# Transfer landing times in a build-time planner: two queues that share one rate, and the loads of units 3 to 5 put around the four quarters of w_out

## The chip, the cores and the metric

The kernel runs on one core of a Trainium2 chip. The metric is the device time in microseconds (us) of one execution; eight timed runs of the kernel before have a median of 397.88 us and lie between 396.91 and 398.88. The profile is one further reading of such an execution, with its own time.

## The reference

Attention with a squared relu, followed by a feed-forward layer with a squared relu:

```python
def _attn_ref(q, k, v):                       # q, k, v: (8, 12, 448, 64), float32
    scores = np.matmul(q, k.transpose(0, 1, 3, 2)) / np.sqrt(64)
    attn = np.maximum(scores, 0.0) ** 2 / 448
    return np.matmul(attn, v)

x = attn_out.transpose(0, 2, 1, 3).reshape(3584, 768)
h = x @ w_in                                  # w_in: (768, 2048)
r = np.maximum(h, 0.0)
out = (r * r) @ w_out                         # w_out: (2048, 768), out float32
```

## The kernel before, in words

**Units and rounds.** The 8 batches of 12 heads are cut into 24 units of four heads. For a unit, q and k are each loaded as one tile `raw` of 448 KB (float32), cast to half precision into a tile `blk`, and turned (transposed) into a tile `qkt`. v is loaded with a cast on the way into a tile `vs`. A unit has 7 rounds; a round multiplies 64 rows of k with all of q (four matmuls, L406, into `sp`), takes the relu with a scale (`rel`: L433 on VectorE or L436 on ScalarE) and squares it (`at`: L440 on ScalarE or L442 on GpSimd). When the seven rounds of a unit are there, 28 matmuls with v (L471) follow, and their results are copied to `xt`. In a batch's feed-forward part, L533 multiplies `xt` with w_in, L522 (ScalarE) and L517 (VectorE) form the squared relu `g`, and L682 or L747 multiply g with w_out and store.

**Units 0 to 2, the first batch.** They come first and are cut into two column parts, so that the first product with w_in (L582, four groups of six matmuls, one for each quarter of w_in) can start early. The q and k of units 1 and 2 are loaded by GpSimd into a g buffer. Up to planned time 45 the planner puts small idle matmuls (L885) where TensorE would have nothing to do.

**w_in and w_out.** Each comes in four quarters of 768 KB (counted in half precision), loaded by GpSimd (L380 and L385). The quarters of w_out are `w2[0][0]`, `w2[0][1]`, `w2[1][0]`, `w2[1][1]`. After the first batch's feed-forward part, `combine_w2` forms four differences of them, t1 to t4, each in two halves (L708 on GpSimd, L711 on VectorE); they serve a product of two row blocks with seven half-size multiplications in place of eight (L747). Every half of t1 waits for all four quarters, and t2 to t4 come behind t1.

**Who issues what.** SyncE's queue carries the raw tiles (L302), the transposing transfers of units 6 and up (L361) and the output stores (L628). GpSimd's queue carries v (L375), w_in and w_out. A queue issues in order; an instruction that has to wait holds all that stand behind it on its engine.

**The planner.** All operations are first added to a `Plan`, with costs, due times, and sometimes a time `after` which they may start. `Plan.run` simulates engines, buffers and transfers, always takes the ready operation with the earliest due time for an engine that is free, and emits the instructions in that order. The chip then runs each engine's instructions in the emitted order, and waits only on semaphores: a planned time exists only in the planner. Where a raw load has `gate=True`, a tiny memset on GpSimd (L299) stands ahead of it, and through it the load can't start before GpSimd gets there. The planner has no model of the port that VectorE and GpSimd share beyond L711 and L726 waiting for a free GpSimd. Before the change, all transfers run one after the other through a single server:

```python
if size:
    dma = max(dma, begin + 1.2) + size / 390e3
    op.end = dma + 1.0
```

**The buffers that matter here.** There are 4 raw tiles, 3 blk, 6 qkt, 4 vs, 4 rel, 11 at, and 4 banks `mm` of PSUM. A raw tile is free for the next load when its cast (L325) is done; a blk tile when it has been turned.

Of the kernel before, what the change touches and what calls it, by code (L numbers as in the profile page):

```python
# [42 lines left out]
class Plan:  # L43
# [27 lines left out]
        return op  # L71

    def run(self):
        n_ops = len(self.ops)
        late: dict = {}
        for z, op in enumerate(self.ops):
            op.id = z
            op.wait = len(op.deps)
            op.ready = op.after
        for op in reversed(self.ops):  # L80
            if not op.fixed or op.alts[0][0] != "PE":
                took = min(a[2] for a in op.alts)
                if len(op.alts[0]) > 4 and op.alts[0][4]:
                    took = 7.0
                due = min([x.due for x in op.nexts] or [1e6]) - took - 0.1
                op.due = due if op.due is None else min(op.due, due)
        waiting: list = []
        for op in self.ops:
            if not op.wait:
                insort(waiting, (op.due, op.id, op))  # L90
        events = sorted({0.0} | {op.after for op in self.ops} | set(self.busy.values()))
        heapq.heapify(events)
        mode, dma, done = None, 0.0, 0
        last = None
        while done < n_ops:
            if not events:
                raise RuntimeError("no operation can go on")
            now = heapq.heappop(events)
            while events and events[0] <= now + 1e-9:
                heapq.heappop(events)  # L100
            again = True
            while again:
                again = False
                for eng in ("PE", "ACT", "DVE", "POOL", "SP"):
                    if self.busy[eng] > now + 1e-9:
                        continue
                    got = None
                    if eng == "PE" and last is not None and last.glue is not None:
                        soon = self.soon(last.glue)
                        if now < soon <= now + 0.45:  # L110
                            heapq.heappush(events, soon)
                            continue
                        if soon <= now:
                            got = waiting.index((last.glue.due, last.glue.id, last.glue)), (
                                last.glue.alts[0])
                    got = got or self.pick(eng, now, waiting)
                    if got is None:
                        if eng == "PE" and now < self.fill_until:
                            self.fill(now)
                            heapq.heappush(events, self.busy[eng])  # L120
                        continue
                    z, alt = got
                    op = waiting.pop(z)[2]
                    _, busy, took, emit, *rest = alt
                    begin = now
                    size = rest[0] if rest else 0
                    if eng == "PE":
                        last = op
                        begin += self.SWITCH.get((mode, op.mode), 0.0)
                        mode = op.mode  # L130
                        if now < self.cold:
                            busy, took = busy * 1.6, took * 1.6
                    if len(rest) > 1 and self.busy["POOL"] > now:
                        wait = self.busy["POOL"] - now
                        busy, took = busy + wait, took + wait
                    op.engine, op.start = eng, begin
                    op.end = begin + took
                    self.busy[eng] = begin + busy
                    if size:
                        dma = max(dma, begin + 1.2) + size / 390e3  # L140
                        op.end = dma + 1.0
                        if eng == "POOL":
                            self.sent += [op.end] * (2 if size == 458752 and took > 1.0 else 1)
                    if len(rest) > 1:
                        self.busy["POOL"] = max(self.busy["POOL"], self.busy[eng])
                    for b in op.bufs:
                        if b.tile is None:
                            slot = min(x for x in self.pools[b.pool] if x[0] <= now + 1e-9)
                            self.pools[b.pool].remove(slot)
                            b.tile, b.slot = slot[2], slot[1]  # L150
                    emit()
                    heapq.heappush(events, self.busy[eng])
                    seen = op.end + self.LAG[eng]
                    for b in op.bufs:
                        b.left -= 1
                        b.end = max(b.end, op.end + 0.07)
                        if not b.left:
                            self.pools[b.pool].append((b.end, b.slot, b.tile))
                            heapq.heappush(events, b.end)
                    for x in op.nexts:  # L160
                        x.wait -= 1
                        x.ready = max(x.ready, seen)
                        if not x.wait:
                            insort(waiting, (x.due, x.id, x))
                            heapq.heappush(events, x.ready)
                    done += 1
                    again = True
        return max(op.end for op in self.ops)

    def soon(self, op):  # L170

# [11 lines left out]
    def fill(self, now):  # L183

        free = [x for x in self.pools["mm"] if x[0] <= now + 1e-9]
        if len(free) > 1:
            slot = min(free)
            self.filler(slot[2])
            self.pools["mm"].remove(slot)
            self.pools["mm"].append((now + 0.2, slot[1], slot[2]))  # L190
        self.busy["PE"] = now + 0.11
# [26 lines left out]
def kernel(  # L218
# [68 lines left out]
    def load_qk(n, w, after=0.0, gate=False):  # L287
        b, u = divmod(n, NU)
        buf = Buf("raw")

        def tile_of():
            return buf.tile

        src = (q if w == "q" else k)[b, 4 * u:4 * u + 4].rearrange(
            "(f e) (p t) d -> (e p) f (t d)", e=2, t=TJ)
        deps = []
        if gate:
            deps.append(plan.add(
                [("POOL", 0.1, 0.1, lambda: nc.gpsimd.memset(buf.tile[0:1, 0, 0:1], 0.0))],  # L299
                bufs=[buf], after=after))  # L300
# [57 lines left out]
    def turn_dma(n, w, cast):  # L358
        op, blk, _ = cast
        to = Buf("qkt")  # L360
        done = plan.add([("SP", 1.3, 5.0, lambda: nc.sync.dma_start_transpose(  # L361
            out=to.tile, in_=blk.tile.rearrange("p t c -> p (t c)")), 1000000)], [op], [blk, to])
        qkt[n, w] = [done], to

    vst: dict = {}
# [583 lines left out]
    tile(1, rounds[1:2])  # L949
    for w_ in "kq":  # L950
        casts[3, w_] = cast_qk(3, w_, raws[3, w_])
        raws[4, w_] = load_qk(4, w_, 24.0, True)
    load_v(3, 26.0)
    w2_ops = [[load_w2(hf, z, 29.0 + 6.0 * hf + z) for z in range(2)] for hf in range(2)]
    for w_ in "kq":
        raws[5, w_] = load_qk(5, w_, 35.0, True)
    load_v(4, 36.0)
    for i in range(2, STREAM):
        tile(1, rounds[i:i + 1])
        if i % 4 == 3:  # L960
# [11 lines left out]
    def coming(n):  # L972
        return plan.now + 4.5 * (TJ * n - 2 * i) / 2

    skipped, chain = 0, None
    for i in range(STREAM // 2, NB):
        rs = [divmod(r, TJ) for r in range(max(STREAM, 2 * i), 2 * i + 2)]
        for n in range(NU, NUN):
            if i == max(STREAM // 2, TJ * (n - 2) // 2 + 1):
                if n > 5:  # L980
                    for w in "kq":
                        raws[n, w] = load_qk(n, w, coming(n) - 26.0)
                if n > 4:
                    load_v(n, coming(n) - 6.0)
            if i == max(STREAM // 2, (TJ * (n - 1) + 1) // 2 - 2) and n > 3:
                for w in "kq":
                    casts[n, w] = cast_qk(n, w, raws[n, w])
                if n < NPE:
                    for w in "kq":
                        turn_pe(n, w, casts[n, w])  # L990
                else:
                    for w in "kq":
                        turn_dma(n, w, casts[n, w])
# [60 lines left out]
```

## Time and profile before

| | |
|---|---|
| median of 8 timed runs | 397.88 us |
| profiled execution, its own time | 398.88 us |
| its span in the trace | 397.1 us (1.8 us lie around it) |
| TensorE busy | 382.4 us, 96% of the span |
| VectorE, ScalarE, GpSimd busy | 267.4, 279.9 and 175.9 us |
| mean granted TensorE clock | 0.991 |
| read from and written to HBM | 45.61 and 11.01 MB |

TensorE is busy nearly always, so what can be won or lost is what it does not work, and where it works at a lower clock. "Releaser" in the profile's rows is what ended an idle time. Times in the rows are counted from the start of the span.

### The profile page before, as it was taken

The page shows a single profiled execution, that of the slowest core. Times are in us where ns is not written, and L with a number is a line of the kernel's source. Part 1 is how long each engine was busy: PE and PEld are TensorE (multiplying, and loading weights), DVE is VectorE, ACT ScalarE, POOL GpSimd, SP SyncE. Part 2 cuts the span into 40 slices and gives each one's busy share as a digit, 9 for nine tenths or more (in the row PEclk, how much of TensorE's full clock was granted, in tenths as well). Part 3 has the DMA queues.
Part 4 walks back from the last instruction along what each step waited for, and adds up shares of the span by engine and source line. Part 5 has one row for each costly group of instructions (what it writes and reads, how often), then busy time and mean ns, then how long its engine had stood idle before and what let it go on. Part 6 is the DMA issues. An engine that isn't in the chain of part 4 may idle for free.

```text
span 397.1 us, 8331 instructions
## 1 busy us (share of the span) xinstructions
PE 382.4 (96%) x3298; PEld 202.0 (51%) x3298; DVE 267.4 (67%) x382; ACT 279.9 (70%) x417; POOL 175.9 (44%) x174
## 2 busy tenths in 40 slices
PE   8997996999999999999999999999999999999996
PEld 4543663444445544544555545544555445555563
DVE  2663888867688657767797655858686767355841
ACT  3985998699876788758878877879586876244111
POOL 7564579548474346448613645335411533000100
PEclk9998999899999999999999999999999999999999
DMA  9999999695937837667587596384263001220143
GB/s 192 191 235 252 267 240 169 113 191 118 235 70 191 192 69 154 165 166 118 126 182 172 119 196 151 73 205 118 45 129 81 2 1 30 62 50 1 41 115 85
DMA packets 69671, 52.72 MB, mean 133 GB/s; under 512 B 36864, under 2 KB 69632, under 8 KB 69632
## 3 DMA queue, kind: packets, MB, share of 16 engines
q1 hardware_dynamic: 53744, 38.61, 39.4%
q0 software_dynamic: 15296, 12.72, 22.0%
q10 hardware_dynamic: 592, 0.85, 0.6%
q8 instruction: 26, 0.43, 0.5%
q14 instruction: 13, 0.11, 0.1%
HBM read 45.61 MB, written 11.01 MB: 143 GB/s over the span
## 4 chain that ended last, share of the span: by engine, by line
PE 82%; DMA 8%; ACT 3%; DVE 2%; issue 2%; POOL 1%; POOLq 0%; DVEq 0%
PE mm L533 35%; PE mm L747 27%; PE sp L406 8%; PE mm L471 7%; DMA w<-in_moe_w_in_dram 6%; PE mm L682 3%; DMA g<-in_q_dram 2%; ACT rel L436 1%; DVE comb L726 1%; ACT g L522 1%; ACT at L440 1%; PE mm L582 1%; DVE g L517 1%; POOL g L315 1%; PE mm L345 1%
## 5 line engine op out<-in xcount | busy, mean ns | idle before, releaser
L533 PE MATMUL mm<-xt,w 128*128 128x448 f16 (+1 forms) x768 | 149.0, 346 | 0.0
L442 POOL TENSOR_TENSOR at<-rel 128x896 f16<-128x896 f32 (+1 forms) x48 | 77.8, 1622 | 108.9 <-ACT rel L436 82.4
L440 ACT ACTIVATE at<-rel 128x896 f16<-128x896 f32 (+1 forms) x120 | 109.6, 930 | 9.7 <-DVE rel L433 5.0
L517 DVE SCALAR_TENSOR_TENSOR g<-mm,g 128x448 f16<-128x448 f32 (+1 forms) x128 | 76.3, 604 | 52.3 <-ACT g L522 52.1
L433 DVE TENSOR_SCALAR rel<-sp 128x896 f32<-128x896 f32 (+3 forms) x87 | 90.9, 1048 | 27.8 <-PE sp L406 25.9
L533 PEld LDWEIGHTS <-w 128*128 128x128 f16 x768 | 72.3, 98 | 69.8 <-issue 11.4
L522 ACT ACTIVATE g<-mm 128x448 f16<-128x448 f32 (+1 forms) x128 | 67.1, 534 | 41.3 <-PE mm L533 40.5
L436 ACT ACTIVATE rel<-sp 128x896 f32<-128x896 f32 (+2 forms) x87 | 77.9, 900 | 7.9 <-PE sp L406 6.4
L325 POOL CAST blk<-raw 128x896 f16<-128x896 f32 x42 | 40.9, 984 | 40.6 <-issue 19.5
L747 PEld LDWEIGHTS <-comb 128*128 128x128 f16 x416 | 39.7, 98 | 31.3 <-issue 4.2
L406 PE MATMUL sp<-qkt,qkt 64*64 64x448 f16 (+2 forms) x756 | 51.7, 340 | 0.6 <-ACT rel L436 0.3
L666 ACT ACTIVATE part<-mm 128x384 f32<-128x384 f32 x44 | 21.5, 488 | 40.8 <-PE mm L747 36.2
L759 DVE SCALAR_TENSOR_TENSOR part<-mm,part 128x384 f32<-128x384 f32 x52 | 28.5, 554 | 24.7 <-ACT part L666 12.7
L747 PE MATMUL mm<-w,comb 128*128 128x384 f16 x208 | 37.0, 326 | 1.0 <-DVE part L668 1.0
L747 PE MATMUL mm<-wt,comb 128*128 128x384 f16 x208 | 37.0, 326 | 0.2 <-DVE comb L726 0.2
L471 PE MATMUL mm<-at,vs 64*64 64x448 f16 (+1 forms) x672 | 35.9, 343 | 0.0
L747 PEld LDWEIGHTS <-g 128*128 128x128 f16 x264 | 25.1, 98 | 19.2 <-issue 3.0
L406 PEld LDWEIGHTS <-qkt 64*64 64x64 f16 x756 | 17.3, 105 | 27.7 <-issue 24.4
L375 POOL DMA_DIRECT2D vs<-in_v_dram x48 | 29.9, 630 | 2.6 <-DMA g<-in_q_dram 1.5
L747 PE MATMUL mm<-w,g 128*128 128x384 f16 x176 | 30.8, 326 | 0.0
L471 PEld LDWEIGHTS <-vs 64*64 64x64 f16 x756 | 22.3, 106 | 13.2 <-issue 3.7
L648 POOL COPY rest<-g 128x1024 f16<-128x1024 f16 x8 | 8.9, 1108 | 36.0 <-DVE g L517 36.0
(56 smaller groups left out, 228.1 us busy)
## 6 DMA issues: line engine op xcount, KB each, us to landing
out_dram<-part SPq DMA_DIRECT2D x108, 96.0 KB, 2.2
raw<-in_k_dram SPq DMA_DIRECT2D x22, 448.0 KB, 4.1
raw<-in_q_dram SPq DMA_DIRECT2D x21, 448.0 KB, 5.0
vs<-in_v_dram POOLq DMA_DIRECT2D x48, 112.0 KB, 3.7
w<-in_moe_w_in_dram POOLq DMA_DIRECT2D x4, 768.0 KB, 15.0
w<-in_moe_w_out_dram POOLq DMA_DIRECT2D x4, 768.0 KB, 14.1
qkt<-blk SPq DMA_TRANSPOSE x36, 3.9
raw<-in_q_dram ACTq DMA_DIRECT2D x1, 448.0 KB, 4.5
```

Of the source, the lines that this page charges most:

```text
L325: return lambda: fn(blk.tile.rearrange("p t (f d) -> p f t d", f=2), tile_of().rearrange("p f (t d) -> p f t d", d=D))
L375: nc.gpsimd.dma_start(out=buf.tile[64 * r:64 * r + 64], in_=src[:, u, hs])
L406: nc.tensor.matmul(sp[64 * c:64 * c + 64, e, c0:c0 + w].rearrange("p (t c) -> p t c", c=TP), lhsT=kT[r, t, 64 * e:64 * e + 64], rhs=qT[r, ...
L433: dve(n, lambda: nc.vector.tensor_scalar(out=rel(), in0=sp.tile[:, :, 0:width], scalar1=0.0, scalar2=SK, op0=ALU.max, op1=ALU.mult)),
L436: act(n, lambda: nc.scalar.activation(out=rel(), in_=sp.tile[:, :, 0:width], func=AF.Relu, scale=SK))],
L440: act(n, lambda: nc.scalar.activation(out=dst(), in_=rel(), func=AF.Square)),
L442: lambda: nc.gpsimd.tensor_mul(dst(), rel(), rel()))],
L471: nc.tensor.matmul(banks[f].tile[64 * e:64 * e + 64, c0:c0 + w], lhsT=vs[r, e ^ c, t * D:(t + 1) * D], rhs=a[r, e, :], start=(t == 0), sto ...
L517: nc.vector.scalar_tensor_tensor(out=dst, in0=src, scalar=0.0, in1=dst, op0=ALU.is_gt, op1=ALU.mult)
L522: nc.scalar.activation(out=dst, in_=src, func=AF.Square)
L533: nc.tensor.matmul(bank.tile[:, c0:c0 + w], lhsT=w1[f // 4][:, m, f % 4 * P:(f % 4 + 1) * P], rhs=xts[b].tile[:, m, cols], start=(m == 0), ...
L747: nc.tensor.matmul(buf.tile[:, 0:HALF], lhsT=lhs()[:, j, :], rhs=w[:, j, :], start=(first and j == 0), stop=(j == NH - 1), skip_group_chec ...
```

## The change

The planner gets a second model of transfers. `run` now simulates five times. After each simulation, `land` takes every transfer with its start and its queue (SyncE's, ScalarE's or GpSimd's), lets the queues that have something under way share 400 KB/us equally, serves each queue in order, and records when each transfer lands; the next simulation uses these landing times. Only the order of the last simulation is emitted. The transposing transfers count 600000 bytes in place of 1000000.

The loads of units 3 to 5 get other places. Unit 4's raw loads move from planned time 24 to 20 and unit 5's from 35 to 25. v of unit 3 comes at 20 in place of 26. The w_out quarters, planned at 29, 30, 35 and 36 before, now come at 26, 30, 34 and 34, with v of unit 4 ahead of the second quarter and v of unit 5 (loaded later before) ahead of the third. The raw loads of units 6 and up may not start before planned time 50.

```diff
+        for _ in range(5):
+            self.pools = {name: list(slots) for name, slots in start[0].items()}
+            self.busy, self.sent, self.order = dict(start[1]), [], []
...
+            self.simulate()
+            self.land()
+        for emit in self.order:
+            emit()
...
+    def land(self):
+        queues: dict = {}
+        for op in sorted((op for op in self.ops if op.size), key=lambda op: op.start):
+            queues.setdefault(op.engine, deque()).append([op.start + 1.2, op.size, op])
+        now = 0.0
+        while queues:
+            live = [q for q in queues.values() if q[0][0] <= now + 1e-9]
...
+            rate = 400e3 / len(live)
+            step = min(q[0][1] / rate for q in live)
...
+                if q[0][1] <= 1e-3:
+                    self.landing[q.popleft()[2].id] = now + 0.8
...
-                    if size:
-                        dma = max(dma, begin + 1.2) + size / 390e3
-                        op.end = dma + 1.0
+                    if op.size:
+                        op.end = max(begin + 2.2 + op.size / 390e3, self.landing.get(op.id, 0.0))
...
-            out=to.tile, in_=blk.tile.rearrange("p t c -> p (t c)")), 1000000)], [op], [blk, to])
+            out=to.tile, in_=blk.tile.rearrange("p t c -> p (t c)")), 600000)], [op], [blk, to])
...
-        raws[4, w_] = load_qk(4, w_, 24.0, True)
-    load_v(3, 26.0)
-    w2_ops = [[load_w2(hf, z, 29.0 + 6.0 * hf + z) for z in range(2)] for hf in range(2)]
-    for w_ in "kq":
-        raws[5, w_] = load_qk(5, w_, 35.0, True)
-    load_v(4, 36.0)
+    for n in (4, 5):
+        for w_ in "kq":
+            raws[n, w_] = load_qk(n, w_, 5.0 * n, True)
+    load_v(3, 20.0, 20.0)
+    w2_ops = [[load_w2(0, 0, 26.0, 26.0)], []]
+    load_v(4, 27.0, 27.0)
+    w2_ops[0].append(load_w2(0, 1, 30.0, 30.0))
+    load_v(5, 32.0, 32.0)
+    w2_ops[1] += [load_w2(1, z, 34.0, 34.0) for z in range(2)]
...
-                        raws[n, w] = load_qk(n, w, coming(n) - 26.0)
-                if n > 4:
+                        raws[n, w] = load_qk(n, w, max(50.0, coming(n) - 26.0))
+                if n > 5:
```

More of the change, by code (lines that the diff above doesn't have):

```diff
@@ L73, in run @@
     def run(self):
-        n_ops = len(self.ops)
-        late: dict = {}
         for z, op in enumerate(self.ops):
             op.id = z
-            op.wait = len(op.deps)
-            op.ready = op.after
         for op in reversed(self.ops):
@@ L86, in run, with simulate @@
                 op.due = due if op.due is None else min(op.due, due)
+        start = {name: list(slots) for name, slots in self.pools.items()}, dict(self.busy)
+        uses = [(b, b.left) for b in {b for op in self.ops for b in op.bufs}]
+        self.landing: dict = {}
+        for _ in range(5):
+            self.pools = {name: list(slots) for name, slots in start[0].items()}
+            self.busy, self.sent, self.order = dict(start[1]), [], []
+            for b, left in uses:
+                b.left, b.end, b.tile = left, 0.0, None
+            self.simulate()
+            self.land()
+        for emit in self.order:
+            emit()
+        return max(op.end for op in self.ops)
+    def land(self):
[5 more added lines that the diff above has]
+            live = [q for q in queues.values() if q[0][0] <= now + 1e-9]
+            if not live:
+                now = min(q[0][0] for q in queues.values())
+                continue
+            rate = 400e3 / len(live)
+            step = min(q[0][1] / rate for q in live)
+            later = [q[0][0] - now for q in queues.values() if q[0][0] > now + 1e-9]
+            step = min([step] + later)
+            now += step
+            for q in live:
+                q[0][1] -= rate * step
+                if q[0][1] <= 1e-3:
+                    self.landing[q.popleft()[2].id] = now + 0.8
+            queues = {name: q for name, q in queues.items() if q}
+    def simulate(self):
+        for op in self.ops:
+            op.wait, op.ready, op.engine, op.size = len(op.deps), op.after, None, 0
         waiting: list = []
@@ L92, in run @@
         heapq.heapify(events)
-        mode, dma, done = None, 0.0, 0
+        mode, done = None, 0
         last = None
-        while done < n_ops:
+        while done < len(self.ops):
             if not events:
@@ L125, in run @@
                     begin = now
-                    size = rest[0] if rest else 0
+                    op.size = rest[0] if rest else 0
                     if eng == "PE":
@@ L138, in run @@
                     self.busy[eng] = begin + busy
-                    if size:
-                        dma = max(dma, begin + 1.2) + size / 390e3
-                        op.end = dma + 1.0
+                    if op.size:
+                        op.end = max(begin + 2.2 + op.size / 390e3, self.landing.get(op.id, 0.0))
                         if eng == "POOL":
-                            self.sent += [op.end] * (2 if size == 458752 and took > 1.0 else 1)
+                            self.sent += [op.end] * (2 if op.size == 458752 and took > 1.0 else 1)
                     if len(rest) > 1:
@@ L150, in run @@
                             b.tile, b.slot = slot[2], slot[1]
-                    emit()
+                    self.order.append(emit)
                     heapq.heappush(events, self.busy[eng])
@@ L167, in run @@
                     again = True
-        return max(op.end for op in self.ops)
     def soon(self, op):
@@ L187, in fill @@
             slot = min(free)
-            self.filler(slot[2])
+            self.order.append(lambda: self.filler(slot[2]))
             self.pools["mm"].remove(slot)
```

## The prediction

> **What bounds the kernel now.** First the page's slices and its chain: TensorE is busy 96% of the span and carries 82% of the chain, so the time changes only where TensorE idles or is clocked down. The first two rows below say where: in slice 4 and in slices 7 and 8 (each 9.93 us), beside the two ends.
>
> ```profile
> PE   8997996999999999999999999999999999999996
> PEclk9998999899999999999999999999999999999999
> PE 82%; DMA 8%; ACT 3%; DVE 2%; issue 2%; POOL 1%; POOLq 0%; DVEq 0%
> ```
>
> Then the timeline of TensorE for both places. The bracket is the idle time before the row and its releaser.
>
> ```profile
> 28.95 1.46 PE L582 MATMUL mm<-w,xt 128*128 128x512 f16 x6 [0.70 <-DMA w<-in_moe_w_in_dram]
> ...
> 36.63 2.72 PE L582 MATMUL mm<-w,xt 128*128 128x512 f16 x6 [2.25 <-DMA w<-in_moe_w_in_dram]
> ```
>
> The last quarter of w_in lands at 36.6. The six matmuls that waited 2.25 us for it take 2.72 us, the six before 1.46: the clock was halved after the idle time. The second place:
>
> ```profile
> 65.93 0.38 PE L406 MATMUL sp<-qkt,qkt 64*64 64x448 f16 x4 [0.31 <-ACT rel L436]
> 70.11 4.44 PE L682 MATMUL mm<-w,g 128*128 128x384 f16 x16 [3.79 <-DVE g L517]
> ```
>
> TensorE waits 3.79 us for the last g masks of VectorE; the 16 matmuls then take 4.44 us, the next 16 take 2.77. What VectorE and GpSimd did:
>
> ```profile
> 63.52 6.14 DVE L711 TENSOR_TENSOR wt<-w,w 128x1536 f16<-128x1536 f16 x1
> 69.58 0.87 DVE L517 SCALAR_TENSOR_TENSOR g<-mm,g 128x320 f16<-128x320 f32 x2
> ```
>
> ```profile
> 61.84 2.69 POOL L325 CAST blk<-raw 128x896 f16<-128x896 f32 x3
> 64.47 1.25 POOL L375 DMA_DIRECT2D vs<-in_v_dram  x2
> 65.71 3.12 POOL L708 TENSOR_TENSOR wt<-w,w 128x1536 f16<-128x1536 f16 x1
> ```
>
> The half of t1 on VectorE takes 6.14 us; later L711 operations take 0.95. GpSimd worked without a gap from 61.84 to 68.83, and VectorE came through at its end (68.83 + 0.85 = 69.68). The two g masks stand behind it. So this meeting costs 3.8 us of idle TensorE and 1.7 us (4.44 - 2.77) of halved clock.
>
> Between the two places ScalarE sets the pace (25.95 of 26.30 us busy):
>
> ```profile
> 40.00:66.30 26.30, 25.88 (x309) 16.31 (x308) 22.11 (x32) 25.95 (x43) 19.26 (x22) 1.00 1.08 234
> ```
>
> **Transfers.** Alone, GpSimd's queue moved 1.23 MB in 18 to 24 us (205 KB per us), and SyncE's 0.70 MB in 44 to 46 (350). From 26 to 35 they ran together and moved 0.88 and 1.63 MB: 0.88/0.205 + 1.63/0.350 = 8.95 of 9 us. So the two queues take turns in one resource, and bytes can be added as time.
>
> ```profile
> q0 software_dynamic: 4414, 3.36, 85.0%
> q1 hardware_dynamic: 1633, 2.75, 32.0%
> ```
>
> These are both queues from 36.6 to 62.3, MB in the second column: 16.4 + 7.9 = 24.3 of 25.7 us. The transfer view gives the quarters of w_out 11.6 us to landing for the third (issued at 44.16), and 14.4 as the mean of the last two; so the last one, issued at 45.05, took 17.2 and landed at 62.25. VectorE reached t1 1.3 us after that.
>
> **The change, part by part.** The emitted order of both programs, engine by engine, shows the following.
>
> *Start.* Unit 1's k is now turned ahead of unit 0's tiles, its q ahead of the first scores. That q is issued at 2.34 and took 6.8 us: 9.14. With the turn (0.58 us) the scores start near 9.7 in place of 8.71, 1.0 us later. The 0.70 and 2.25 us at w_in cover it, else it would cost 1.0. I take 0.
>
> *w_in.* Nothing moves ahead of its quarters in GpSimd's queue. All four gating memsets of units 3 and 4 come behind the third product in the queue, near 23.2 (21.8 and 25.0 before): unit 3's loads slow w_in 1.3 us later, unit 4's 2 us earlier. I take 36.6 again, with 0.5 us to either side.
>
> *Between the last L582 and the first L682.* All scores of the first batch now stand ahead of the last L582 group, under the wait for w_in. Behind it TensorE has 12 score matmuls of 320 columns fewer (0.99 us), 7 turns fewer (0.56) and 3 idle matmuls fewer (0.38). ScalarE, which sets the pace, has two rel (0.70) and two at (0.74) of 320 columns fewer, one at of 448 fewer (0.95), one rel of 448 (0.92) and one turn's copy (0.90) more: -2.9 + 0.9 = -2.0 us. VectorE loses one rel and two copies (-2.3); GpSimd gets one product (1.67) and one cast (0.93) more. So this stage ends 2.0 us earlier. Bounds: 0, if unit 3's turned k, now ahead of six of these scores, makes them late (its load, issued 1.3 us later, lands near 31.0, its cast ends near 32); 2.9, if only ScalarE's losses count. TensorE would have nothing left at 64.3, and VectorE would be at t1 at 61.5.
>
> *The landing that t1 waits for.* v of unit 5 (0.229 MB, 1.1 us) now goes ahead of the last two quarters, and v of unit 4 ahead of the second; this fills about 0.5 us of the 1.4 us in which neither queue moved. That gives 62.25 + 0.6 = 62.9. The raw loads of units 6 and 7 are planned from 50 on, but they have no gate: SyncE issues each as soon as its raw tile's cast is done, some 4 us earlier than before, and the same bytes are through by 62. Unit 6's cast then also comes earlier, so that its turning transfer (5.4 us to landing in this trace) and unit 8's k (0.459 MB, 1.3 us) run beside the last quarter: up to 2.5 us more. Landing between 62.9 and 65.4; I take 64.2, the middle, since only unit 6's turn is sure to run by then. So t1 waits 2.7 us on VectorE where it waited for nothing, and behind it wait the same two g masks, a rel, and TensorE.
>
> *The meeting with GpSimd.* Its order there is a product, two casts, v of unit 6, a cast that waits for unit 6's turn, and only then its half of t1. At 64.2 it is in v of unit 6 or in the gap behind it, so VectorE gets through at once or after 1.25 us; I take 0.3. The half of t1 ends at 64.2 + 0.3 + 0.95 = 65.5, and L682 starts 0.45 us behind that as now (70.11 - 69.66), near 66.0. At the other end VectorE waits for GpSimd's 3.12 us as well, and L682 starts at 68.7.
>
> The Trainium skill, "SBUF — State Buffer", section "SBUF: two separate sides", has a rule here: the port pair is an exclusive lock, and whoever starts first holds it for one whole instruction. The row of 6.14 us goes further, as VectorE let five GpSimd instructions pass. By the page a meeting costs one GpSimd instruction at most, and L682 would start between 65.6 and 68.7; the row leaves more than 68.7 possible.
>
> *The clock.* TensorE would idle from 64.3 to 66.0, 1.7 us. After 0.70 us it kept its clock, after 2.25 it lost it. 1.7 is nearer to 2.25, so I take the 1.7 us of loss as staying; kept, they are a gain of 1.7.
>
> The page "TensorE: Matmul & The Clock Gate", section "What's actually happening", lets the clock fall only after an idle window of about 3.4 us. By that rule the loss would go and the sum be 1.7 us lower; the 2.25 us before 36.63 were shorter than such a window and did lower it.
>
> *Behind it.* One half of t3 moves from GpSimd (3.09 us) to VectorE (0.95), between g masks, where TensorE never idles now; other reorderings stand where TensorE lost only 1.0 us between 100 and 360. I take +0.2, bounds -1.0 and +2.0.
>
> **Sum.** L682 starts at 66.0 in place of 70.11, -4.1, which holds the 2.0 us of the stage before; clock 0; behind it +0.2: -3.9. The profiled execution would go from 398.88 (span 397.1 and 1.8 around it) to 395.0. It lies 1.0 above the median of the runs, which would go from 397.88 to 394.0.
>
> **Rivals.** *Landed in time, clock kept:* the last quarter comes by 62.9, L682 starts near 64.6, and 1.7 us of clock are won: -5.5 - 1.7 + 0.2 = -7.0, 390.9. For it speaks that bytes alone give 62.9; against it, unit 6's turn. *The meeting stays:* VectorE asks just as GpSimd starts its half of t1, and L682 starts at 68 to 70, so that the stage's 2.0 us are eaten: 396.0 to 398.0. *Slower:* the ungated loads and turns push the last quarter past about 65.5, where GpSimd stands ready at its own half. Both halves start together, GpSimd wins, and L682 starts at landing + 3.1 + 0.95 + 0.45: at 66.5 this is 71.0, or +0.9 and +0.2, 399.0; at 68 it is 400.5. For it speaks that the planner holds those loads back only in its own time; against it, that the same bytes took until 62.25 with idle stretches.
>
> **Chances.** A measurement can tell about 0.2% (0.8 us) from no change. Forecast, 392.4 to 395.5: 0.45. Landed in time: 0.18. The meeting stays: 0.15, of which 0.07 are still faster by over 0.2%. Slower: 0.22. So faster 0.45 + 0.18 + 0.07 = 0.70, same 0.08, slower 0.22. The range 390.0 to 399.6 leaves out some 0.05 of the second case and 0.11 of the last.
>
> **What would show it.** In the changed profile L582's last group starts at 36.1 to 37.1; the first L533 near 42 in place of 44.80; VectorE's wait ahead of the first L711 names a w_out transfer, and that L711 takes under 2.3 us; L682 first starts near 66. A first L711 of 4 us or more, or L682 past 70, would make the prediction wrong. So would a start of L533 past 44, or a new idle time of TensorE over 1 us behind 75.

## The result, and the profile after

The changed kernel takes 394.39 us (median of 11 runs, 392.81 to 395.16) beside 397.35 us for the kernel before on the same chip: a ratio of 0.9916, with a 95% interval of 0.9898 to 0.9933. By this ratio it is faster by 3.3 us (the two medians lie 3.0 us apart); the forecast was 3.9, and 394.0 us. The profiled execution took 394.14 us, 4.74 less than that of before; its mean granted clock was 0.994 (0.991 before).

The slices and the chain of the page after:

```profile
PE   8898999999999999999899999999999999999995
PEclk9998999999999999999999999999999999999999
...
PE 84%; ACT 6%; DVE 4%; DMA 2%; issue 2%; POOL 1%; DVEq 0%; ACTq 0%; POOLq 0%
```

The dent in slices 7 and 8 has gone, and the second dent of the clock with it. What is left is one 8 in slice 4, and a new 8 in slice 20. Lines after the edited planner are numbered higher in this kernel: L582 is now L616, L682 L716, L711 L745, L708 L742, L325 L359, L406 L440, L726 L760, L747 L781. The timeline of TensorE at both places:

```profile
32.31 0.93 PE L379 MATMUL mm<-ident,blk 128*128 128x128 f16 x7 [1.83 <-POOL blk L359]
...
38.54 1.46 PE L616 MATMUL mm<-w,xt 128*128 128x512 f16 x6
...
64.70 0.38 PE L440 MATMUL sp<-qkt,qkt 64*64 64x448 f16 x4 [0.23 <-ACT rel L470]
65.02 2.77 PE L716 MATMUL mm<-w,g 128*128 128x384 f16 x16
```

The first product with w_out starts at 65.02 in place of 70.11 and takes 2.77 us in place of 4.44. The first place has changed its releaser: TensorE waits for the cast of unit 3's k, not for w_in. Its seven turns (0.93 us) ran at the halved clock: the clock record has 0.5 from 32.17 to 35.59, and nowhere else until the end. Before, it had 0.5 from 36.32 to 39.73 and from 70.45 to 73.87.

VectorE at t1, and GpSimd beside it (L409 is the "v issue": the two instructions with which GpSimd starts loads of v):

```profile
62.29 0.95 DVE L745 TENSOR_TENSOR wt<-w,w 128x1536 f16<-128x1536 f16 x1
63.15 0.48 DVE L551 SCALAR_TENSOR_TENSOR g<-mm,g 128x320 f16<-128x320 f32 x1
```

```profile
60.58 1.81 POOL L359 CAST blk<-raw 128x896 f16<-128x896 f32 x2
62.33 1.27 POOL L409 DMA_DIRECT2D vs<-in_v_dram  x2
63.62 0.93 POOL L359 CAST blk<-raw 128x896 f16<-128x896 f32 x1
64.51 3.11 POOL L742 TENSOR_TENSOR wt<-w,w 128x1536 f16<-128x1536 f16 x1
```

The half of t1 takes 0.95 us where it took 6.14. GpSimd's own half no longer stands directly behind the v issue: a cast lies between.

### The profile page after: what moved, and what is told of

The parts are those of the page before. It is cut to its first block, busy times and chain, and to the rows that moved or that the text cites. A ratio compares the mean times of both kernels' runs of the same rounds, so it can differ in the third digit from the quotient of the medians.

```text
span 392.2 us, 8342 instructions
## 1 busy us (share of the span) xinstructions
PE 381.2 (97%) x3304; PEld 201.0 (51%) x3304; DVE 269.0 (69%) x389; ACT 277.0 (71%) x414; POOL 170.0 (43%) x170
## 4 chain that ended last, share of the span: by engine, by line
PE 84%; ACT 6%; DVE 4%; DMA 2%; issue 2%; POOL 1%; DVEq 0%; ACTq 0%; POOLq 0%
PE mm L567 34%; PE mm L781 30%; PE sp L440 9%; PE mm L505 7%; ACT rel L470 2%; DMA raw<-in_k_dram 2%; PE mm L716 1%; ACT at L474 1%; DVE rel L467 1%; PE mm L916 1%; ACT g L556 1%; PE mm L919 1%; DVE wt L745 1%; DVE comb L760 1%; ACT comb L474 1%
## 5 line engine op out<-in xcount | busy, mean ns | idle before, releaser
L567 PE MATMUL mm<-xt,w 128*128 128x448 f16 (+1 forms) x768 | 149.2, 346 | 0.0
L474 ACT ACTIVATE at<-rel 128x896 f16<-128x896 f32 (+1 forms) x123 | 112.1, 932 | 9.7 <-PE mm L505 6.3
L476 POOL TENSOR_TENSOR at<-rel 128x896 f16<-128x896 f32 (+1 forms) x45 | 73.3, 1629 | 97.2 <-ACT rel L470 57.6
L467 DVE TENSOR_SCALAR rel<-sp 128x896 f32<-128x896 f32 (+3 forms) x93 | 96.6, 1043 | 19.6 <-PE sp L440 16.9
L567 PEld LDWEIGHTS <-w 128*128 128x128 f16 x768 | 72.2, 98 | 70.6 <-issue 12.4
L470 ACT ACTIVATE rel<-sp 128x896 f32<-128x896 f32 (+2 forms) x81 | 73.2, 906 | 9.3 <-PE sp L440 5.7
L359 POOL CAST blk<-raw 128x896 f16<-128x896 f32 x42 | 40.6, 975 | 54.5 <-issue 22.3
L781 PEld LDWEIGHTS <-comb 128*128 128x128 f16 x416 | 39.0, 98 | 32.1 <-issue 5.2
L440 PE MATMUL sp<-qkt,qkt 64*64 64x448 f16 (+2 forms) x756 | 52.0, 341 | 2.0 <-ACT rel L470 0.7
L781 PE MATMUL mm<-wt,comb 128*128 128x384 f16 x208 | 37.0, 326 | 1.2 <-DVE comb L760 1.2
L781 PE MATMUL mm<-w,comb 128*128 128x384 f16 x208 | 37.0, 327 | 0.0
L781 PEld LDWEIGHTS <-g 128*128 128x128 f16 x264 | 25.3, 98 | 18.9 <-issue 2.5
L440 PEld LDWEIGHTS <-qkt 64*64 64x64 f16 x756 | 17.5, 105 | 30.0 <-issue 27.4
L781 PE MATMUL mm<-w,g 128*128 128x384 f16 x176 | 30.7, 326 | 0.0
L409 POOL DMA_DIRECT2D vs<-in_v_dram x48 | 29.8, 627 | 1.2 <-DMA g<-in_q_dram 0.7
L682 POOL COPY rest<-g 128x1024 f16<-128x1024 f16 x8 | 9.6, 1197 | 36.8 <-DVE g L551 36.8
```

The source lines that it names most:

```text
L359: return lambda: fn(blk.tile.rearrange("p t (f d) -> p f t d", f=2), tile_of().rearrange("p f (t d) -> p f t d", d=D))
L409: nc.gpsimd.dma_start(out=buf.tile[64 * r:64 * r + 64], in_=src[:, u, hs])
L440: nc.tensor.matmul(sp[64 * c:64 * c + 64, e, c0:c0 + w].rearrange("p (t c) -> p t c", c=TP), lhsT=kT[r, t, 64 * e:64 * e + 64], rhs=qT[r, ...
L467: dve(n, lambda: nc.vector.tensor_scalar(out=rel(), in0=sp.tile[:, :, 0:width], scalar1=0.0, scalar2=SK, op0=ALU.max, op1=ALU.mult)),
L470: act(n, lambda: nc.scalar.activation(out=rel(), in_=sp.tile[:, :, 0:width], func=AF.Relu, scale=SK))],
L474: act(n, lambda: nc.scalar.activation(out=dst(), in_=rel(), func=AF.Square)),
```

## The experiments

Each kernel was compared with runs of the kernel before on the same chip; ratios are to these, with the 95% interval. The experiments ran on three chips, so runs of different rows are compared by their ratios. A stretch of halved clock lasts 3.41 us and lowers the mean clock of a run by 3.41 / 2 / 392 = 0.0044, so the mean clock of each run counts them: about 0.996 is one, 0.991 two, 0.987 three. By that count the kernel before had one to three in its later comparisons, never none; the changed kernel had one in 9 of 12 executions, the profiled one among them (393.7 to 395.2), and none to speak of in 3 (392.8 to 393.1).

| kernel | median us | ratio | interval |
|---|---|---|---|
| the change | 394.39 | 0.9916 | 0.9898 to 0.9933 |
| e1 model alone | 402.68 | 1.0101 | 1.0049 to 1.0153 |
| e2 moved loads alone | 393.23 | 0.9894 | 0.9854 to 0.9933 |
| e3 before, t1 on GpSimd | 391.85 | 0.9864 | 0.9824 to 0.9903 |
| e4 before, matmuls in the wait | 401.03 | 1.0097 | 1.0062 to 1.0131 |
| e5 model, w_out at the new times | 398.78 | 1.0049 | 1.0024 to 1.0074 |
| e6 moved loads, t1 on GpSimd | 392.96 | 0.9902 | 0.9868 to 0.9936 |
| e7 change, t1 on GpSimd | 396.34 | 0.9998 | 0.9974 to 1.0023 |
| e8 change, unit 3 loaded earlier | 392.62 | 0.9906 | 0.9873 to 0.9939 |
| e9 change, last two quarters swapped | 393.57 | 0.9929 | 0.9905 to 0.9954 |
| e10 before, t1 on VectorE | 391.37 | 0.9880 | 0.9841 to 0.9919 |
| e11 before, t1 to t4 on GpSimd | 389.06 | 0.9815 | 0.9780 to 0.9850 |
| e12 change, unit 3 earlier, t1 to t4 on GpSimd | 392.09 | 0.9902 | 0.9864 to 0.9940 |

### Which half of the change brings the gain: e1, e2, e5

e1 takes the change without its last hunk: the new planner, the loads placed as before.

> The planner of the changed kernel with the loads placed as before. In this program both halves of t1 stand on VectorE behind three part evictions, not among the g masks that the first L682 group waits for, so no half of t1 can hold the g masks up. Theory one (the gain is the removed meeting of VectorE's half of t1 with GpSimd, 3.8 us of idle TensorE, and the clock that TensorE keeps, 1.7 us): the first L682 group has under 1 us of idle time ahead of it and takes 2.77 us instead of 4.44; the time falls by 3 to 6 us against the kernel before, to 392 to 395. Rival (the moved loads bring the gain, through an earlier w_in and a shorter stage): the time stays within 1 us of the kernel before, 397 to 399, and L682 starts at 69 to 71.

It became slower by 1.0%. The profiled execution, 398.84 us, is one of two that took 398.6 to 398.8; the other four took 402.6 to 403.2 at about the same mean clock, and no trace shows what they lost. In the profile, no half of t1 holds the g masks now, and L716 starts at 64.27. But behind it TensorE waits 4.45 us. The timelines of TensorE and of GpSimd:

```profile
64.27 2.77 PE L716 MATMUL mm<-w,g 128*128 128x384 f16 x16
71.50 0.93 PE L440 MATMUL sp<-qkt,qkt 64*64 64x448 f16 x8 [4.45 <-ACT rel L470]
```

```profile
57.44 1.26 POOL L409 DMA_DIRECT2D vs<-in_v_dram  x2
67.93 0.93 POOL L359 CAST blk<-raw 128x896 f16<-128x896 f32 x1 [9.23 <-DMA raw<-in_k_dram]
68.82 1.67 POOL L476 TENSOR_TENSOR at<-rel 128x896 f16<-128x896 f32 x1
```

A cast waits 9.23 us for its raw tile, and the product behind it in GpSimd's queue frees a rel buffer that ScalarE and then TensorE need. Theory one was right on the place it named and wrong on the time; the rival was wrong on both.

e2 is the other half: before's planner, the last hunk alone.

> The loads placed as in the changed kernel, with the planner of before. That planner now puts both halves of t1 earlier: VectorE's ahead of four g masks instead of two, GpSimd's behind a row of products and casts. Theory one: the placement alone does not take the meeting away; VectorE's half of t1 takes 3 us or more, or waits for its quarter, and TensorE idles 2 us or more ahead of the first L682 group with the clock halved behind; the time is 396 to 400. Rival (the moved loads bring the gain): VectorE's half of t1 takes 0.95 to 1.6 us, L682 starts at 65 to 67, and the time is 392 to 395.

```profile
58.09 3.71 DVE L711 TENSOR_TENSOR wt<-w,w 128x1536 f16<-128x1536 f16 x1
61.73 1.27 DVE L517 SCALAR_TENSOR_TENSOR g<-mm,g 128x320 f16<-128x320 f32 x3
```

The meeting is still there, as theory one said, but at 58.09, 5.4 us earlier, when TensorE has other work until 61.25. TensorE waits 1.01 us for it, keeps its clock, and starts L682 at 64.56. So the price of a meeting is what stands behind it, and the rival's time came by another road. All six runs had a clock of 0.999 or 1.0.

e5 gives e1 the new times of the w_out quarters alone:

```diff
-    w2_ops = [[load_w2(hf, z, 29.0 + 6.0 * hf + z) for z in range(2)] for hf in range(2)]
+    w2_ops = [[load_w2(0, 0, 26.0, 26.0), load_w2(0, 1, 30.0, 30.0)],
+              [load_w2(1, z, 34.0, 34.0) for z in range(2)]]
```

> The changed kernel's planner, with the raw and v loads placed as before and only the quarters of w_out given the planned times of the changed kernel (26, 30, 34, 34 in place of 29, 30, 35, 36, with the same numbers as due times). Theory two (the planner's model alone lost time because GpSimd issued the w_out quarters some 10 us late, at 39.84 to 43.72, the queues then stood nearly empty, and a later cast waited 9.2 us for its raw tile with a product behind it that TensorE needed): the first quarter is issued before 32, no GpSimd cast waits over 3 us between 55 and 75, TensorE's idle time of 4.45 us behind the first L716 group is gone, and the time is 391 to 395. Rival (the order of loads, not w_out's issue, makes that wait): a wait of TensorE of 2 us or more stays between 60 and 80 and the time is 397 or more.

The quarters left at 27.3 to 40.6, no cast waited over 1.5 us between 55 and 75, and the 4.45 us are gone, as theory two said; but the time, 398.78 us, is the rival's: it came back only half of the way to the kernel before. Against the profile of the changed kernel it is even until 48 us and 3.7 us behind at 66.7, where the timeline of TensorE has:

```profile
50.41 0.56 PE L379 MATMUL mm<-ident,blk 128*128 128x128 f16 x7 [1.65 <-POOL blk L359]
...
66.66 0.38 PE L440 MATMUL sp<-qkt,qkt 64*64 64x448 f16 x4 [1.23 <-DVE rel L467]
```

Between 46.9 and 54.5 four casts in a row waited for raw tiles (2.26, 1.59, 1.26 and 1.95 us): the loads of the coming units are late. So the moved loads are what brings the gain. The new model by itself costs 1.0% (most of it in the runs that have no trace), and with the moved loads it adds nothing: the change's ratio is 0.0022 above that of e2, inside the intervals, and at equal clock (0.999 to 1.0) both take about 393.0.

### Is it the meeting: e3, e10, e6, e7, e9

e3 takes VectorE's way away from t1 in the kernel before (in the list of ways of each half, L711):

```diff
-                            nc.vector.tensor_sub(*args(r)), 0, True)],
+                            nc.vector.tensor_sub(*args(r)), 0, True)][slice(0, 1) if name == "t1" else slice(0, 2)],
```

> The kernel before, with both halves of t1 on GpSimd and none on VectorE. Theory one: VectorE has nothing between the g masks, L682 starts at 66 to 67 instead of 70.11, the 16 matmuls take 2.77 us, and the time falls by 3 to 5.5 us (392.5 to 395). Rival (TensorE would wait for the g masks or for ScalarE's rows all the same, the meeting lies beside another wait): L682 starts at 69 or later and the time falls by less than 1 us. A second price is open: GpSimd spends 3.1 us more ahead of the casts of unit 7, which may cost up to 3 us later.

391.85 us, 0.9864: without any change to loads or planner this wins more than the change. L682 starts at 63.02, takes 2.77 us, and the clock is never halved until the end; L682 and the time both lie below what was written down. Some 3 us of the 7 between the two profiles are not the meeting's: with the same order up to there, the last L582 group started at 34.80 here (36.63 in the profile of before), and the clock was kept behind it. The next meeting is in this trace too: a half of t2 on VectorE takes 5.76 us at 64.58, and TensorE idles 1.07 us at 74 to 75, 0.65 of it for a rel behind that half. VectorE, then GpSimd:

```profile
64.58 5.76 DVE L711 TENSOR_TENSOR wt<-w,wt 128x1536 f16<-128x1536 f16 x1
```

```profile
64.27 1.25 POOL L375 DMA_DIRECT2D vs<-in_v_dram  x2
65.51 3.12 POOL L708 TENSOR_TENSOR wt<-w,w 128x1536 f16<-128x1536 f16 x1
```

Here VectorE asks in a v issue and is not let in until GpSimd's half behind it has ended.

e10 does the opposite and takes GpSimd's way away (`slice(1, 2)`).

> The kernel before, with both halves of t1 on VectorE, the second far behind the first, and GpSimd's place behind the v issue taken by a half of t2, which has to wait for VectorE's t1. Theory one (VectorE gets through at the first instant in which GpSimd starts nothing): VectorE's half of t1 is through when the v issue ends, so it takes 3 us instead of 6.14, L682 starts about 3 us earlier than 70.11, and the time falls by 2 to 4.5 us, to 392.5 to 395. Rival (VectorE's hold has a length of its own, or GpSimd's half of t1 was not what held it): L711 takes 6 us again and the time is within 1 us of the kernel before.

391.37 us, 0.9880, below the range written down; L682 starts at 63.28. In this profile too the last L582 group started early (35.05) and the clock was kept behind it. This is the cleanest of the runs: TensorE and ScalarE have the order of before to the end. GpSimd's place behind the v issue holds a half of t2, which waits for VectorE's t1. Up to there it is the kernel before; so is e4 below, whose L716 is L711 and whose L713 is L708. Timelines of VectorE and GpSimd, first e4, then e10:

```profile
60.81 6.12 DVE L716 TENSOR_TENSOR wt<-w,w 128x1536 f16<-128x1536 f16 x1
```

```profile
59.11 2.69 POOL L325 CAST blk<-raw 128x896 f16<-128x896 f32 x3
61.74 1.25 POOL L375 DMA_DIRECT2D vs<-in_v_dram  x2
62.98 3.12 POOL L713 TENSOR_TENSOR wt<-w,w 128x1536 f16<-128x1536 f16 x1
```

```profile
60.54 1.82 DVE L711 TENSOR_TENSOR wt<-w,w 128x1536 f16<-128x1536 f16 x1
```

```profile
58.85 2.70 POOL L325 CAST blk<-raw 128x896 f16<-128x896 f32 x3
61.48 1.25 POOL L375 DMA_DIRECT2D vs<-in_v_dram  x2
62.73 3.13 POOL L708 TENSOR_TENSOR wt<-w,wt 128x1536 f16<-128x1536 f16 x1
```

Both ask in the second of three casts. In e10 VectorE is through at 62.37, in the v issue; in e4 it stays shut out through the same v issue and through GpSimd's half behind it, and is through at 66.93. The one difference nearby on these two engines is that in e4 GpSimd's half has its operands. That half, ready behind the v issue, is what made 6 us; the expected 3 us were still too many, since the v issue itself keeps nobody out. The changed kernel (62.29) and e9 (63.00) came through at v issues that have a cast behind them.

e6 puts t1 on GpSimd in e2.

> The moved loads with the planner of before, and both halves of t1 on GpSimd. In the moved loads alone VectorE's half of t1 took 3.71 us (0.95 where nothing is in its way) and TensorE waited 1.01 us for the g masks behind it, with the clock kept. Theory one: with nothing to meet, that 1.01 us goes; 391.5 to 393 beside 393.2. Rival: the 3.1 us more on GpSimd make its casts late, and the time is 393.5 to 396.

392.96 against 393.23, 0.9902 against 0.9894: the 1.01 us is gone from the profile, and what it was worth is inside the scatter of the runs. Two of the six took 398.6; their mean clock (0.994 and 0.995) shows one halved stretch, which explains only part of that. Little to win was expected, and little was won; theory and rival are not told apart by the time.

e7 puts t1 on GpSimd in the changed kernel.

> The changed kernel with both halves of t1 on GpSimd. There VectorE's half of t1 took 0.95 us, so theory one expects no gain from taking it away: L716 starts within 1 us of 65.0, and the time is 392.5 to 395.5 (the changed kernel: 394.4). If the changed kernel's g masks were still held up by t1 the time would fall as it did in the kernel before, by 3 us or more, to 391 or less.

396.34 us, by the ratios 0.8% slower than the change. L716 starts at 65.41, as expected; what is new is a later meeting, with a rel behind it. VectorE, then TensorE:

```profile
70.61 5.58 DVE L745 TENSOR_TENSOR wt<-w,wt 128x1536 f16<-128x1536 f16 x1 [0.84 <-POOL wt L742]
```

```profile
77.25 0.48 PE L440 MATMUL sp<-qkt,qkt 64*64 64x448 f16 x4 [2.33 <-DVE rel L467]
```

The clock halves behind that wait. No gain was expected and none came; the time lies 0.8 us above the range written down. A meeting can be moved as well as removed.

e9 swaps the issue of the last two quarters in the changed kernel; nothing else moves on any engine.

```diff
-    w2_ops[1] += [load_w2(1, z, 34.0, 34.0) for z in range(2)]
+    w2_ops[1] += [load_w2(1, z, 34.0, 34.0) for z in (1, 0)]
```

> The changed kernel with its last two w_out quarters issued in the other order, everything else in the same order on every engine. t1 subtracts the first quarter from the third; with the swap the one it needs lands last, near 62.5 instead of 58.6. Theory (t1 waits only for its own two quarters, and in the changed kernel VectorE came in at 62.29, in time before GpSimd's next instructions): now VectorE's wait ahead of the first L745 names a w_out transfer. If VectorE then comes in before GpSimd's v issue (62.33), L716 stays within 1 us of 65.0 and the time within 0.5 us of 394.4; if it comes in during the v issue, it is held to the end of the cast (64.5) or of GpSimd's own half (67.6), L716 starts at 66.5 to 70, and the time is 396 to 399. Rival, the prediction's step (t1 waits for all four quarters anyway): nothing changes, 394.4 within 0.5.

VectorE, then GpSimd:

```profile
63.00 0.95 DVE L745 TENSOR_TENSOR wt<-w,w 128x1536 f16<-128x1536 f16 x1
```

```profile
63.03 1.27 POOL L409 DMA_DIRECT2D vs<-in_v_dram  x2
64.28 0.96 POOL L359 CAST blk<-raw 128x896 f16<-128x896 f32 x1
```

Now the semaphore that t1 waits on is the last quarter's, which lands at 62.87. This costs VectorE no idle time, since it is in a g mask until 63.08: the half of t1 starts at 63.00, 0.03 us ahead of the v issue, it takes 0.95 us, and L716 starts at 65.73. The ratio (0.9929) is the change's within the intervals, and the median lies 0.3 us below what was written down; the time does not tell theory and rival apart. The landings do: in the changed kernel the last quarter landed at 62.48, after t1 had begun at 62.29. So t1 waits for its own two quarters alone: `w2[1][0]` and `w2[0][0]`.

### The clock and unit 3: e4, e8

e4 was to keep the clock up in the kernel before, with the wait left in: 36 small matmuls ahead of the first L682 group, in the group's own bank.

```diff
+                    for _ in range(36 if warm else 0):
+                        plan.filler(bank.tile)
```

> The kernel before, with 36 small matmuls (128 by 256, into the group's own bank, overwritten by the group) ahead of the first L682 group, so that TensorE works through the time in which it waits for the g masks. The meeting stays. Theory one: the first 16 matmuls of L682 take 2.77 us instead of 4.44, L682 starts within 0.5 us of 70.1, and the time falls by 1.2 to 2.0 us. Rival (4.44 us comes from late operands or a queue, not from the clock): they take 4.4 us again and the time stays within 0.5 us.

The wait could not be filled, since the bank they write is freed by the very g masks:

```profile
67.38 6.75 PE L890 MATMUL mm<-part 128*128 128x256 f16 x36 [3.77 <-DVE g L517]
73.96 2.76 PE L686 MATMUL mm<-w,g 128*128 128x384 f16 x16
```

They came behind the wait of 3.77 us, on the path, and the time rose by 1.0%. Yet the row below answers the question: once the clock was up again, the same 16 matmuls took 2.76 us. The 4.44 us were the clock.

e8 lets unit 3's raw loads of the changed kernel start at planned time 17.

```diff
-        raws[3, w] = load_qk(3, w, 20.0, True)
+        raws[3, w] = load_qk(3, w, 17.0, True)
```

> The changed kernel with the raw loads of unit 3 planned from 17 on instead of 20. In the changed kernel unit 3's k left at 23.37, its cast waited for it, and TensorE idled 1.83 us at 30.5 to 32.3 with the clock halved from 32.17 to 35.59. Theory three (this wait and its half clock took 1 to 3 us of the change's gain): the gating memsets stand ahead of two products, the loads leave about 1.5 to 3 us earlier, no idle time over 1 us stays between 28 and 34, and the time falls by 1 to 3 us, to 391.5 to 393.5. Rival (ScalarE's pace between 40 and 65 eats whatever is won ahead of it, or w_in lands later by as much): within 0.7 us of the changed kernel. In this program t1 also comes behind the g masks on VectorE.

Unit 3's k left at 17.88 in place of 23.37, and the wait at 32.31 is gone; another of 1.34 us stands ahead of 28.78, behind the cast of unit 3's q, which had waited 1.79 us for its tile. That one did not halve the clock:

```profile
PEclk9999999999999999999999999999999999999999
```

392.62 us, by the medians 1.8 below the change; the ratios (0.9906 and 0.9916) do not tell the two apart. In the profiles the early wait and its halved stretch are worth only 0.8 us of it: the last L567 group ahead of the first L716 starts at 60.05 in place of 60.84. The lead is 1.0 us at the first L716 (63.99 and 65.02) and 1.8 at the last L781 matmul, and e8 also has t1 in another place, behind the g masks. What one halved stretch costs is read better from the change's own runs: 394.4 with one, 393.0 without.

### The best version: e11, e12

e11 gives all eight halves of t1 to t4 to GpSimd in the kernel before, e12 in e8.

```diff
-                            nc.vector.tensor_sub(*args(r)), 0, True)],
+                            nc.vector.tensor_sub(*args(r)), 0, True)][:1],
```

> The kernel before, with all eight halves of t1 to t4 on GpSimd. With t1 alone on GpSimd the time was 391.85 and the next meeting still held VectorE for 5.76 us at 64.58, with 1.1 us of idle TensorE behind it (74 to 75). Theory one (meetings are what costs): that idle time goes too; 390.5 to 392. Rival (GpSimd becomes late: it gets 12 us more between 60 and 100): casts or rest copies come late, and the time is 392.5 to 396.

> The changed kernel with unit 3's raw loads planned from 17 on (392.6 alone) and all eight halves of t1 to t4 on GpSimd. Theory one: idle time of TensorE between 60 and 85 is below 0.5 us in all, and the time is 390.5 to 392.5. Rival (GpSimd late): 393 to 396, with waits of TensorE on GpSimd's casts or rest copies.

e11 takes 389.06 us (388.84 to 389.24): 1.85% below the kernel before, by the ratios 1.0% (4 us) below the change, under the range of theory one. Its L682 groups stand without a gap; the row of 5.37 us is two groups in one:

```profile
62.99 2.77 PE L682 MATMUL mm<-w,g 128*128 128x384 f16 x16
65.69 0.68 PE L406 MATMUL sp<-qkt,qkt 64*64 64x448 f16 x8
66.31 5.37 PE L682 MATMUL mm<-w,g 128*128 128x384 f16 x32
```

e12 is level with it until 100 us (0.1 us apart) and loses 2.3 us by 195, most of it at one place: an L760 of VectorE takes 2.75 us at 187.60, beside a copy and a cast of GpSimd, and TensorE waits 1.73 us for it. At the end e12 is 3.0 us behind. Its median, 392.09, is in theory one's range; two of its ten runs took 396.7, untraced. With the meetings over t1 to t4 gone on both sides, the moved loads and the new planner win nothing; most of what decides between the two profiles is one later meeting.

## Why the prediction was right, step by step

The time came out within 0.4 us. The place was right, and so was the mechanism, a meeting of VectorE and GpSimd with a halved clock behind it. But several terms were wrong, and that they cancelled was luck.

*Start.* Scores began at 9.30 in place of 8.71, covered, as said.

*w_in: the term that failed first.* It said 36.6 again; the last quarter landed at 33.1. Part of this is chance: with the order of before it landed at 34.7 in e11. Yet the last L582 group started at 38.54, outside of 36.1 to 37.1. The text had named the cause, a cast of unit 3's k that ends near 32 (it ended at 32.26), but had given it only the price of a stage that ends no earlier. It cost 1.83 us of wait and a halved clock. What this was worth is known in part: by the change's own runs a halved stretch costs 1.4 us (394.4 and 393.0), and e8, without either, is 0.8 us ahead by the last L567 group before L716.

*The stage up to L682.* VectorE reached t1 at 62.29 in place of 63.52, 1.2 us earlier and not 2.0 (61.5).

*The landing: the step that was wrong.* The forecast had t1 wait 2.7 us, from 61.5 until the last quarter would land at 64.2. Its price for the landing was too high: unit 6's turn and unit 8's k did run beside the last quarter (issued at 59.02 and 60.41), yet it landed at 62.48, and VectorE came only at 62.29. So a wait for all four quarters would have cost 0.2 us. And there was none: "every half of t1 waits for all four quarters" is true of the planner's list of dependencies alone. On the chip t1 waits on the semaphores of the two tiles that it reads; these had landed at 41.81 and 58.56. In e9, where one of the two lands last, at 62.87, VectorE still lost nothing. The slower rival needed the last quarter past 65.5, and hung on the same dependency.

*The meeting.* 0.95 us and 0.3 were forecast, 0.95 was measured, at a v issue as assumed. But the reason was thin: by e10 and e4 a v issue lets VectorE through if GpSimd's ready half does not stand behind it, and here a cast stood there. No run puts that half directly behind the v issue in the changed kernel. L716 started at 65.02 and not at 66.0.

*The clock.* It was to stay lost at L682. It was kept there (2.77), 1.7 us won, and one of the two halved stretches remained, at unit 3's k.

*Behind it.* +0.2 was forecast, within -1.0 and +2.0. By the end of the first L682 group the change was ahead by 6.8 us (74.55 to 67.79); at the start of the last L747 matmul by 4.86 (392.80 to 387.95). So 1.9 us went, close to the outer bound. The rows are VectorE's halves of t2 and t4 at 69.43 to 73.58, stretched beside GpSimd's casts (2.55 us for two, 1.68 for one), with 0.46 us of idle TensorE at 76.80; two L760 of 1.52 and 1.41 us at 191 to 194, with 1.04 us; and 0.36 us at 247.91. On the other side, before's own idle 1.01 us at 118 is gone. Some 1 us of the loss was not traced to a row. The 1.04 us are one of the signs that the prediction set against itself.

So the profile went -6.8 + 1.9 = -4.9 (4.74 measured). This is the mechanism of the rival "landed in time, clock kept", with a loss behind it that brought it back to the forecast's number. The profiled run of before lies high among its kind, so the medians differ by only 3.0, and the ratio says 3.3.

The Trainium skill, "SBUF — State Buffer", section "SBUF: two separate sides", gives the shared ports to whoever starts first, for the whole instruction; read by itself, a meeting then costs one instruction. The half of e2 agrees: asked at 58.09 in GpSimd's half (57.90 to 61.00), it was through at 61.80. The halves of before, e3, e4 and e7 (5.58 to 6.14 us) do not; several GpSimd instructions passed. The measurements decide: one instruction is no upper bound here.

The page "TensorE: Matmul & The Clock Gate", section "What's actually happening", lets the clock fall after an idle window of about 3.4 us, in windows that run on freely. The fixed step agrees with the traces here (last section). The idle window does not: the window ahead of the change's halved stretch was busy for 0.50 of its time, around an idle time of 1.83 us.

## What to carry to other kernels

Read what an instruction waits for from its semaphores in the trace, not from the dependency list of a planner that ordered it. Where two engines can shut each other out, look at what stands ready behind them and who waits behind the loser: taking the choice of engine away from eight small operations won 1.85% here, more than the new model and the moved loads together (0.84%), whose gain came by moving such a meeting. And before a gain is put down to a planner's model, run the model and the moved operations apart: here one half cost 1.0% and the other won 1.1%.

## What the runs showed of the hardware

*The clock.* In all fourteen traces, up to 375 us, the halved stretches last 3.41 us or twice that, and all lie on a grid of that step. Laying the grid over TensorE's busy time gives one pattern: a window in which TensorE was busy for 61% or more was never followed by a halved one, one of 46% or less always was, and between these it went both ways (0.48 and 0.53 kept, 0.51 and 0.53 lost). The two halved stretches of the kernel before follow windows busy for 0.43 and 0.10. So an idle time of about 1.8 us costs a further 1.4 us or nothing: the clock was lost behind 1.83 us (the change), 1.86 (e7) and 1.67 (e9), and kept behind 1.79 (e10), 1.73 (e12) and 1.68 (e6). Where an idle time falls in the grid is part of it (e12's lies across two windows, of which the worse was busy for 0.63); what decides near one half no run here tells. By the mean clocks, such steps are also what makes runs of one kernel differ: 394.4 and 393.0 for the change.

*The shared port.* VectorE is not kept out by a v issue (62.29, 61.48 and 63.00), but is kept out through it where GpSimd's half of t1 with its operands stands directly behind (before and e4; in e3 it even asks in the issue, at 64.58, and starts only behind the half). Whether GpSimd takes the port when such an instruction is queued, or VectorE has to wait for something else, no run here tells.
